# Squares of 32x32 transposed by VectorE for the blocks of w3 and for k and q of pairs 3 to 7

## The chip, the cores and the metric

The kernel runs on one core of a Trainium2 chip. The metric is the device time of one execution in microseconds; the time given is the median of three runs. Beside them one more execution was profiled, and every row below is of that one.

## What is computed

The reference has three parts, one after the other. 

```python
q, k, v: (2, 8, 576, 64) float32; omega: (128, 64)
scale = 1.0 / sqrt(sqrt(64)); q_s, k_s = q * scale, k * scale
phi(x) = exp(x @ omega.T - sum(x*x)/2 - max(...)) / sqrt(128)     # the sum falls out against the max
kv = sum_s phi(k_s)[s, m] * v[s, d];  z = sum_s phi(k_s)[s, m]
attn = (phi(q_s) @ kv) / (phi(q_s) @ z + 1e-6)
x = attn with heads side by side: (1152, 512)
x = ((x @ w1) * (x @ w2)) @ w3 @ w_out             # w1, w2: (512, 1024); w3: (1024, 1024); w_out: (1024, 512); float64
out = sum over 4 experts of p[:, e] * (relu(x @ ew1[e]) @ ew2[e])
```

Since `z` and `kv` divide out the constants, only the product of scale, x and omega enters the exponential. `w3 @ w_out` does not depend on the tokens.

## The kernel before

**Attention.** Batch and head give 16 heads of 576 tokens; two heads are a pair, and eight pairs (0 to 7, class `Pair`) go through the program. A pair's 512 main tokens of k and of q are loaded as a tile of 128 rows by 512 numbers (`kr`, `qr`), transposed, and multiplied with omega (`features`, or `features_halves` from pair 5 on), which VectorE's maximum and ScalarE's exponential turn into `ek` and `eq`. Before, the transposing is done by TensorE: `transposed` (L259) issues four transposes of 128x128 against an identity into a bank, and one copy out of the bank, with the multiplication by the scale, by VectorE for k and by ScalarE for q. The loop over pairs (L514) handles in turn n the features of pair n, the attention of pair n - 1, the transposes of pair n + 1 and the loads of pair n + 2. The tokens over 512 of each head are the tails, loaded and handled apart.

**The fold.** Beside the attention, from the table `BESIDE` (L41), the kernel multiplies w3 by w_out in advance: eight blocks (`fold`, L185), each of two units (`fold_transposed`, L174). A unit is a block of 128 by 512 of w3: loaded as float64 words (`from_f64`, one DMA of 512 KB into a tile with three buffers), made float32 by ScalarE (L93) and VectorE (L94, L95), transposed by TensorE into bank `w`, split into a high part (ScalarE) and a low part (VectorE), and then used as weights of 12 matmuls of 512 columns (L195) into bank `po`. Eight blocks of w_out (`load_wo`) are the right side; they come in the same way and are split by ScalarE and GpSimd.

**After it.** `AFTER` lists the products with w1 and w2 (`gated`, L148; their weights by `load_w12`) and the product with the folded matrix (`expert_input`, L204); then come the experts (L834 and on), which the change leaves alone.

**Order.** The framework's scheduler writes one list of instructions for each engine, by priorities and by its own estimate of times; each engine works through its list in order, so an instruction that waits holds up all that stand behind it on its engine. SP's list holds nearly all the loads. A load by SP takes one of eight completion counters in rotation (DMAHW0 to DMAHW7) and waits until the load that had it before, eight loads back, has landed.

Of the kernel before, what the change touches and what calls it, by code (L numbers as in the profile page):

```python
# [8 lines left out]
F32 = mybir.dt.float32  # L9
BF16 = mybir.dt.bfloat16  # L10
F32R = mybir.dt.float32r
U32 = mybir.dt.uint32
ACTF = mybir.ActivationFunctionType
ALU = mybir.AluOpType
AX = mybir.AxisListType

HI, LO = 0, 1
HS_BUFS = 4
O_BUFS = 6
HALVES = 5  # L20
WARM = 6


# [22 lines left out]
def attention_moe_kernel(ctx: ExitStack, tc: tile.TileContext, q, k, v, omega, mw1, mw2, mw3, mwo, probs, ew1, ew2, out):  # L46
    nc = tc.nc
    B, H, S, D = q.shape
    M = omega.shape[0]
    NT, DM = out.shape  # L50
    DFF = mw1.shape[1]
    NE, _, EFF = ew1.shape
    P = 128
    NPAIR = H // 2
    R = 4
    MAIN = P * R
    TAIL = S - MAIN
    assert B * TAIL == P and B == 2 and H * D == DM and 2 * D == P and M == P
    KD = DM // P
    KF = DFF // P  # L60
    KE = EFF // P
    NTILE = NT // P
    HS = S // 2
    SCALE = float(1.0 / D**0.25)
# [10 lines left out]
    def bank(tag):  # L75
        return ps_p.tile([P, 512], F32, tag=tag, name="ps_" + tag, bufs=BANKS[tag])

    def split(hi, lo, src, eng=None):

        nc.scalar.activation(out=hi, in_=src, func=ACTF.Copy)  # L80
        (eng or nc.vector).tensor_tensor(out=lo, in0=src, in1=hi.bitcast(F32), op=ALU.subtract)  # L81

    def from_f64(src, name):


        r = cv.tile([P, 512, 2], U32, tag="f64", name="f64", bufs=3)
        nc.sync.dma_start(out=r.rearrange("p (k c) w -> p k (c w)", k=src.shape[1]), in_=src.bitcast(U32))
        low, high = r[:, :, 0], r[:, :, 1]
        f = cv.tile([P, 512], F32, tag="f64f", name=name, bufs=2)
        e = cv.tile([P, 512], U32, tag="f64e", name="f64e", bufs=2)  # L90
        fb = f.bitcast(U32)

        nc.scalar.activation(out=f, in_=high.bitcast(F32), func=ACTF.Prelu, scale=2.0**-112, alpha=2.0**32)  # L93
        nc.vector.tensor_scalar(out=e, in0=low, scalar1=29, scalar2=None, op0=ALU.logical_shift_right)  # L94
        nc.vector.scalar_tensor_tensor(out=fb, in0=fb, scalar=3, in1=e, op0=ALU.logical_shift_left, op1=ALU.bitwise_or)  # L95
        return f

    def load_w64(pool, src, name, eng):
        f = from_f64(src, name + "f")
        t = pool.tile([P, 2, 512], F32R, tag=pool.name, name=name)  # L100
        split(t[:, HI], t[:, LO], f, eng=eng)
        return t
# [5 lines left out]
    def transpose(out, in_, rows=slice(0, P)):  # L108
        return nc.tensor.transpose(out, in_, ident[rows, rows])
# [3 lines left out]
    om = const.tile([P, 2, M], F32, name="om")  # L113
# [12 lines left out]

    xt = [[xt_p.tile([P, 2, S], F32R, tag="xt", name=f"xt{i}") for i in range(NPAIR)] for _ in range(B)]


    mctx = ctx.enter_context(ExitStack())  # L130
    w1_p = mctx.enter_context(tc.tile_pool(name="w1", bufs=8, side="right"))
    w3_p = mctx.enter_context(tc.tile_pool(name="w3", bufs=1, side="right"))
    cctx = mctx.enter_context(ExitStack())
    cv = cctx.enter_context(tc.tile_pool(name="cv", bufs=2, side="right"))
    w12, hid, wo, w3o, x2, xf = {}, {}, [], [], {}, {}

    def load_w12(g):

        for w, src in enumerate((mw1, mw2)):
            src = src[:, g * P:(g + 1) * P].rearrange("(k p) c -> p k c", p=P)  # L140
            t = load_w64(w1_p, src, "w12", nc.gpsimd)
            w12[w, g] = t.rearrange("p a (k c) -> p a k c", k=KD)

    def load_wo():
        f = len(wo)
        wo.append(load_w64(w1_p, mwo[f * P:(f + 1) * P].unsqueeze(1), "wo", nc.gpsimd))

    def gated(a_p, bufs, b, g, tags):  # L148

# [23 lines left out]

    def fold_transposed(u):  # L174

        m, hf = divmod(u, KF // 4)
        r = from_f64(mw3[m * P:(m + 1) * P, hf * 512:(hf + 1) * 512].unsqueeze(1), "w3f")
        ps = bank("w")
        for g in range(4):
            transpose(ps[:, g * P:(g + 1) * P], r[:, g * P:(g + 1) * P])  # L180
        wt = cv.tile([P, 2, 512], F32R, tag="w3T", name="w3T", bufs=2)
        split(wt[:, HI], wt[:, LO], ps)
        w3T.append(wt)

    def fold(m):  # L185

        po = bank("po")
        n = 0
        for hf in range(KF // 4):
            u = m * (KF // 4) + hf  # L190
            while len(w3T) < min(u + 2, KF * (KF // 4)):
                fold_transposed(len(w3T))
            for g in range(4):
                for a, c in PASSES:
                    nc.tensor.matmul(  # L195
                        out=po, lhsT=w3T[u][:, a, g * P:(g + 1) * P], rhs=wo[hf * 4 + g][:, c],
                        start=(n == 0), stop=(n == 3 * KF - 1),
                    )
                    n += 1
        t = w3_p.tile([P, 2, 512], F32R, tag="w3o", name="w3o", bufs=KF)  # L200
        split(t[:, HI], t[:, LO], po)
        w3o.append(t)
# [51 lines left out]
    with ExitStack() as actx:  # L254
        at = actx.enter_context(tc.tile_pool(name="at", bufs=2))
# [3 lines left out]
        def transposed(r, name, tag="t"):  # L259

            ps = bank(tag)
            for g in range(4):
                transpose(ps[:, g * P:(g + 1) * P], r[:, 2 * g:2 * g + 2].rearrange("p r d -> p (r d)"))
            t = at.tile([P, 512], F32, tag=name, name=name)
            if name == "kT":
                nc.vector.tensor_scalar(out=t, in0=ps, scalar1=SCALE, scalar2=None, op0=ALU.mult)
            else:
                nc.scalar.activation(out=t, in_=ps, func=ACTF.Copy, scale=SCALE)
            return t

        ended = []
# [51 lines left out]
        def raw_tile(name, bufs=2):  # L323
            return at.tile([P, 2 * R, D], F32, tag=name, name=name, bufs=bufs)
# [5 lines left out]
        ps = bank("po")  # L330
        for n in range(WARM):
            nc.tensor.matmul(out=ps, lhsT=zeros[:, :P], rhs=zeros, start=True, stop=True)
# [4 lines left out]
        ps = bank("x")  # L337
        om_first = transpose(ps[:, :M], om_raw.rearrange("m j d -> m (j d)")).ins
        for j in range(2):
            s = slice(j * D, (j + 1) * D)  # L340
            nc.vector.tensor_copy(out=om[s, j], in_=ps[s, :M])
            nc.gpsimd.tensor_copy(out=omh[s], in_=om[s, j])

        va = [st.tile([P, 2 * R, D1], F32, name=f"va{n}") for n in range(2)]
# [3 lines left out]
        for b in range(B):  # L348
            t = st.tile([P, H, D1], F32, name=f"vt{b}")
# [18 lines left out]
        class Pair:  # L368


            def __init__(self, n):
                self.n, self.b, self.i = n, n // NPAIR, n % NPAIR
                self.ek, self.eq, self.eT = [None] * 2, [None] * 2, [None] * 2

            def load_kq(self, q_eng=nc.sync):
                b, i = self.b, self.i
                self.raw = []
                for name, src, eng in (("kr", k, nc.sync), ("qr", q, q_eng)):
                    r = raw_tile(name)
                    eng.dma_start(  # L380
                        out=r.rearrange("p (h r) d -> p h (r d)", h=2),
                        in_=src[b, 2 * i:2 * i + 2, :MAIN, :].rearrange("h (p r) d -> p h (r d)", r=R),
                    )
                    self.raw.append(r)

            def load_v(self):

# [9 lines left out]
                nc.gpsimd.tensor_copy(out=self.va[:, :, :D], in_=self.vr)  # L397

            def transpose_kq(self):
                self.kT = transposed(self.raw[0], "kT")  # L400
                self.qT = transposed(self.raw[1], "qT", "t" if self.n else "et")

# [8 lines left out]
            def features(self, t, e):  # L411
                if self.n >= HALVES:
                    return features_halves(t, e)
# [4 lines left out]
            def of(self, e, j, r):  # L418

                return e[r % 2][:, 2 * j + r // 2] if self.n >= HALVES else e[j][:, r]  # L420

            def kv_sums(self):

                ps = bank("kv")
                for j in range(2):
                    h = 2 * self.i + j
                    for r in range(R + 1):
                        e, a = (self.of(self.ek, j, r), self.va[:, j * R + r]) if r < R else (ekt[:, h], vt[self.b][:, h])
                        nc.tensor.matmul(out=ps[:, j * D1:(j + 1) * D1], lhsT=e, rhs=a, start=(r == 0), stop=(r == R))
                self.kva = at.tile([P, 2, D1], F32, tag="kva", name="kva", bufs=NPAIR + 1)  # L430
                nc.scalar.activation(out=self.kva, in_=ps[:, :2 * D1].rearrange("p (j d) -> p j d", j=2), func=ACTF.Copy)
# [26 lines left out]
        def attend_tail(b, ps_of):  # L458
# [13 lines left out]
            s = TAIL_COLS  # L472
            for i in range(NPAIR):
                transpose(ps[:, i * P:(i + 1) * P], xs[:, 2 * i:2 * i + 2].rearrange("p j d -> p (j d)"))
            for i in range(NPAIR):
                x, c = xt[b][i], i * P + b * TAIL
                split(x[:, HI, s], x[:, LO, s], ps[:, c:c + TAIL])

        pairs = [Pair(n) for n in range(B * NPAIR)]

# [83 lines left out]
    for s in AFTER.split():  # L564
        if s[0] == "w":
            load_w12(int(s[1]))
        elif s[0] == "c":
            if s == "c0":
                cctx.close()
                xq_p = mctx.enter_context(tc.tile_pool(name="xq", bufs=1, reuse_waits="tile", side="right"))  # L570
            expert_input(int(s[1]))
        else:
            gated(a_p, 6, int(s[1]), int(s[2]), ALL_BANKS[int(s[1])])
# [305 lines left out]
```

## Time and profile before

| | |
|---|---|
| median of three runs | 677.01 us (676.75 to 678.62) |
| the profiled execution | 675.28 us, of which its span is 673.5 us |
| TensorE busy in the span | 98% |
| VectorE, ScalarE, GpSimd busy | 67%, 61%, 18% |

The span runs from the first instruction to the last; the 1.8 us left of the execution lie around it. A share is an average over stages: attention and fold (to about 145 us), the products after them (to about 300 us), and the experts.

### The profile page before, as it was taken

To read this page: it belongs to the slowest core of one execution; us is meant where nothing else is said; L and a number is where in the kernel's file an instruction comes from. 1 tells how busy PE (TensorE), PEld (TensorE's weight loads), DVE (VectorE), ACT (ScalarE), POOL (GpSimd) and SP (SyncE) were. 2 spreads that over 40 slices of the span, in tenths; PEclk is the share of its full clock that TensorE was granted. 3 is DMA by queue.
4 is the path that set the end of the run, shared out by engine and by line. 5 is a ranking of instruction groups with operands and counts; after the bars stand their busy time and mean duration, and the time that the engine had idled before them with its cause. 6 is when DMAs were issued, how large, how long until landed. Compare 5 with 4: busy or idle time off the path is not lost.

```text
span 673.5 us, 12392 instructions
## 1 busy us (share of the span) xinstructions
PE 661.3 (98%) x4895; PEld 634.7 (94%) x4895; DVE 448.9 (67%) x754; ACT 414.1 (61%) x895; POOL 123.9 (18%) x145
## 2 busy tenths in 40 slices
PE   8999999999999999999999999999999999999997
PEld 6788888889999999999899999999999998999996
DVE  3867755657462225257968867968689588687795
ACT  5897465574352224237868778768587677687740
POOL 2321000042140000000022141321331312304300
PEclk9999999999999999999999999999999999999999
DMA  9865333156120002002255385592872765737715
GB/s 230 289 204 173 109 111 95 63 176 200 32 64 1 1 1 64 1 1 64 77 143 142 46 145 108 98 154 48 156 142 32 147 120 83 142 75 105 135 44 172
DMA packets 51178, 70.58 MB, mean 105 GB/s; under 512 B 8048, under 2 KB 34160, under 8 KB 51120
## 3 DMA queue, kind: packets, MB, share of 16 engines
q1 hardware_dynamic: 37792, 49.05, 24.3%
q0 software_dynamic: 12640, 20.19, 20.1%
q8 instruction: 38, 0.62, 0.4%
q10 hardware_dynamic: 688, 0.56, 0.2%
q14 instruction: 20, 0.16, 0.1%
HBM read 47.24 MB, written 22.54 MB: 104 GB/s over the span
## 4 chain that ended last, share of the span: by engine, by line
PE 83%; DMA 5%; DVE 4%; issue 3%; ACT 3%; SPq 1%; POOL 0%; DVEq 0%; ACTq 0%; POOLq 0%
PE ps_po L195 6%; PE ps_f L709 6%; PE ps_f L791 5%; PE ps_x L709 3%; PE ps_w L709 3%; PE ps_et L709 3%; PE ps_po L158 3%; PE ps_f L158 3%; PE ps_kv L709 3%; PE ps_po L709 3%; PE ps_kv L791 3%; PE ps_x L791 3%; PE ps_w L158 3%; PE ps_et L791 3%; PE ps_t L709 2%
## 5 line engine op out<-in xcount | busy, mean ns | idle before, releaser
L743 POOL DMA_DIRECT2D out_dram<-o x98 | 81.9, 912 | 355.2 <-DVE o L768 173.0
L81 DVE TENSOR_TENSOR hs<-hd,hs 128x1024 fp32r<-128x1024 f32 x48 | 58.3, 1218 | 1.5 <-ACT hs L80 1.5
L80 ACT ACTIVATE hs<-hd 128x1024 fp32r<-128x1024 f32 x48 | 50.6, 1056 | 5.7 <-DVE hd L605 4.6
L195 PE MATMUL ps_po<-wo,w3T 128*128 128x512 f32 x192 | 48.3, 400 | 0.0
L709 PE MATMUL ps_f<-x,w1e 128*128 128x288 f32 x288 | 46.2, 294 | 0.0
L693 ACT ACTIVATE hd<-hd 128x288 f32<-128x288 f32 x96 | 40.7, 438 | 9.0 <-DVE hd L691 8.5
L605 DVE TENSOR_TENSOR hd<-hd 128x512 f32<-128x512 f32 x64 | 43.9, 686 | 0.8
L605 DVE TENSOR_TENSOR raw<-raw 128x512 f32<-128x512 f32 x64 | 43.9, 686 | 0.5
L791 PE MATMUL ps_f<-w2e,hs 128*128 128x256 f32 x288 | 43.2, 282 | 0.0
L81 DVE TENSOR_TENSOR w2e<-raw,w2e 128x1024 fp32r<-128x1024 f32 x32 | 38.8, 1218 | 5.4 <-ACT w2e L80 5.3
L195 PEld LDWEIGHTS ps_po<-wo,w3T 128*128 128x128 f32 x192 | 34.8, 188 | 7.0
L709 PEld LDWEIGHTS ps_f<-x,w1e 128*128 128x128 f32 x288 | 40.9, 188 | 0.1
L791 PEld LDWEIGHTS ps_f<-w2e,hs 128*128 128x128 f32 x288 | 38.5, 191 | 0.1
L80 ACT ACTIVATE w2e<-raw 128x1024 fp32r<-128x1024 f32 x32 | 33.1, 1054 | 6.3 <-DVE raw L605 3.2
L81 POOL TENSOR_TENSOR w<-w12f,w 128x512 fp32r<-128x512 f32 x16 | 23.5, 1478 | 68.0 <-ACT w L80 68.0
L81 DVE TENSOR_TENSOR w1e<-raw,w1e 128x1024 fp32r<-128x1024 f32 x24 | 29.3, 1219 | 5.8 <-ACT w1e L80 5.7
L158 PE MATMUL ps_po<-xt,w 128*128 128x288 f32 x144 | 32.5, 296 | 0.4 <-DVE w3o L81 0.4
L158 PE MATMUL ps_w<-xt,w 128*128 128x288 f32 x144 | 32.8, 297 | 0.0
L80 ACT ACTIVATE hid<-a 128x288 fp32r<-128x288 f32 x32 | 12.8, 439 | 28.8 <-DVE a L169 28.8
L80 ACT ACTIVATE w1e<-raw 128x1024 fp32r<-128x1024 f32 x24 | 25.4, 1058 | 6.2 <-issue 2.6
L94 DVE TENSOR_SCALAR f64e<-f 128x512 uint32<-128x512 uint32 x40 | 20.6, 520 | 8.4 <-DMA f<-in_moe_w_dram 5.5
L158 PE MATMUL ps_x<-xt,w 128*128 128x288 f32 x96 | 25.8, 297 | 0.0
(272 smaller groups left out, 1769.2 us busy)
## 6 DMA issues: line engine op xcount, KB each, us to landing
f<-in_moe_w_dram SPq DMA_DIRECT2D x32, 512.0 KB, 3.8
raw<-in_moe_w_dram SPq DMA_DIRECT2D x32, 512.0 KB, 5.2
out_dram<-o POOLq DMA_DIRECT2D x56, 256.0 KB, 5.3
out_dram<-o POOLq DMA_DIRECT2D x42, 128.0 KB, 4.8
f<-in_moe_w_out_dram SPq DMA_DIRECT2D x8, 512.0 KB, 6.2
kr<-in_k_dram SPq DMA_DIRECT2D x8, 256.0 KB, 5.3
vr<-in_v_dram SPq DMA_DIRECT2D x8, 256.0 KB, 4.9
o<-out_dram SPq DMA_DIRECT2D x8, 256.0 KB, 3.8
```

Source lines behind the costliest of these rows:

```text
L80: nc.scalar.activation(out=hi, in_=src, func=ACTF.Copy)
L81: (eng or nc.vector).tensor_tensor(out=lo, in0=src, in1=hi.bitcast(F32), op=ALU.subtract)
L94: nc.vector.tensor_scalar(out=e, in0=low, scalar1=29, scalar2=None, op0=ALU.logical_shift_right)
L158: nc.tensor.matmul(out=bs[c][:, :HS], lhsT=w12[w, g][:, x, kk], rhs=xt[b][kk][:, y, c * HS:(c + 1) * HS], start=(kk == 0 and n == 0), stop ...
L195: nc.tensor.matmul(out=po, lhsT=w3T[u][:, a, g * P:(g + 1) * P], rhs=wo[hf * 4 + g][:, c], start=(n == 0), stop=(n == 3 * KF - 1),)
L605: nc.vector.tensor_tensor(out=o, in0=x, in1=y, op=op)
L693: nc.scalar.activation(out=h, in_=src, func=ACTF.Relu)
L709: nc.tensor.matmul(out=ps, lhsT=w1t[a][:, x, kk, g * P:(g + 1) * P], rhs=x2[b, kk][:, y, s], start=(k in "125" and kk == 0 and n == 0), st ...
L743: dma = nc.gpsimd.dma_start(out=out[toks, d], in_=src[rows], **({} if fresh else dict(accum_op=ALU.add))).ins
L791: nc.tensor.matmul(out=ps, lhsT=t[a][:, x, g, j * P:(j + 1) * P], rhs=w2t[b][:, y, g], start=(k in "15" and g == 0 and n == 0), stop=(k in ...
```

## The change

1. Each block of w3 is loaded by four DMAs, one for each group of 32 partitions, each of which takes 32 rows of four column pieces. VectorE's 32x32 transpose of the tile (one instruction for 128x512, within partition groups) then gives the block transposed, and the split reads and writes it with reordered columns. Four TensorE transposes for each unit and their use of bank `w` go. The rows of w3 in a group of weights are others than before, so w_out's blocks are loaded with matching rows, also in four DMAs.
2. k and q of pairs 3 to 7 are loaded by eight DMAs for a tile of 256 KB, in runs of 32 numbers (128 bytes), and transposed by one VectorE instruction from SBUF to SBUF. Pairs 0 to 2 and the tails stay with TensorE.
3. The scale is multiplied into omega once, so the copies out of the banks no longer multiply.
4. Folded blocks alternate between banks `po` and `w`.

```diff
+SQUARES = 3
...
-    def from_f64(src, name):
+    def from_f64(srcs, name):
         r = cv.tile([P, 512, 2], U32, tag="f64", name="f64", bufs=3)
-        nc.sync.dma_start(out=r.rearrange("p (k c) w -> p k (c w)", k=src.shape[1]), in_=src.bitcast(U32))
+        rows = P // len(srcs)
+        for i, src in enumerate(srcs):
+            o = r[i * rows:(i + 1) * rows].rearrange("p (k c) w -> p k (c w)", k=src.shape[1])
+            nc.sync.dma_start(out=o, in_=src.bitcast(U32))
...
     def load_wo():
-        f = len(wo)
-        wo.append(load_w64(w1_p, mwo[f * P:(f + 1) * P].unsqueeze(1), "wo", nc.gpsimd))
+        hf, g = divmod(len(wo), 4)
+        first = [hf * 512 + i * P + g * SQ for i in range(4)]
+        wo.append(load_w64(w1_p, [mwo[f:f + SQ].unsqueeze(1) for f in first], "wo", nc.gpsimd))
...
     def fold_transposed(u):
         m, hf = divmod(u, KF // 4)
-        r = from_f64(mw3[m * P:(m + 1) * P, hf * 512:(hf + 1) * 512].unsqueeze(1), "w3f")
-        ps = bank("w")
-        for g in range(4):
-            transpose(ps[:, g * P:(g + 1) * P], r[:, g * P:(g + 1) * P])
+        rows = mw3[m * P:(m + 1) * P].rearrange("(j r) f -> r j f", r=SQ)
+        first = [hf * 512 + i * P for i in range(4)]
+        r = from_f64([rows[:, :, f:f + P] for f in first], "w3f")
+        t = cv.tile([P, 512], U32, tag="f64e", name="w3t", bufs=2).bitcast(F32)
+        nc.vector.transpose(t, r)
+        t = t.rearrange("p (j g r) -> p g j r", j=4, g=4)
         wt = cv.tile([P, 2, 512], F32R, tag="w3T", name="w3T", bufs=2)
-        split(wt[:, HI], wt[:, LO], ps)
+        hi, lo = (wt[:, x].rearrange("p (g j r) -> p g j r", j=4, g=4) for x in (HI, LO))
+        split(hi, lo, t)
         w3T.append(wt)
 
     def fold(m):
-        po = bank("po")
+        po = bank(("po", "w")[m % 2])
...
             if name == "kT":
-                nc.vector.tensor_scalar(out=t, in0=ps, scalar1=SCALE, scalar2=None, op0=ALU.mult)
+                nc.vector.tensor_copy(out=t, in_=ps)
             else:
-                nc.scalar.activation(out=t, in_=ps, func=ACTF.Copy, scale=SCALE)
+                nc.scalar.activation(out=t, in_=ps, func=ACTF.Copy)
+            return t
+
+        def load_squares(t, src, eng):
+            t = t.rearrange("p n d -> p (n d)").rearrange("p (h g q c) -> p h g q c", h=2, g=2, c=SQ)
+            src = src.rearrange("h (q p g j) (i c) -> h j i p g q c", q=4, g=2, j=2, c=SQ)
+            for n in range(4):
+                for h in range(2):
+                    eng.dma_start(out=t[n * SQ:(n + 1) * SQ, h], in_=src[h, n // 2, n % 2])
+
+        def squares(r, name):
+            t = at.tile([P, 512], F32, tag=name, name=name)
+            nc.vector.transpose(t, r.rearrange("p n d -> p (n d)"))
             return t
...
-            nc.vector.tensor_copy(out=om[s, j], in_=ps[s, :M])
+            nc.vector.tensor_scalar(out=om[s, j], in0=ps[s, :M], scalar1=SCALE, scalar2=None, op0=ALU.mult)
...
+                self.squares = n >= SQUARES
...
+                    if self.squares:
+                        load_squares(r, src[b, 2 * i:2 * i + 2, :MAIN], eng)
+                        continue
...
             def transpose_kq(self):
+                if self.squares:
+                    self.kT, self.qT = (squares(r, name) for r, name in zip(self.raw, ("kT", "qT")))
+                    return
```

**SP's list, from the first w_out block to the loads of pair 3.** In rows of SP's list, `f_...` is the tile of float64 words, and the brackets name what the row waits for. Before, from the load of v of pair 2 on:

```order
L391 DMA vr<-in_v_dram 128x2x256 [waits DMAHW7_49,Pool_49]
L87 DMA f_247<-in_moe_w_out_dram 128x1024 [waits DMAHW0_49]
L87 DMA f_257<-in_moe_w_out_dram 128x1024 [waits DMAHW1_49]
L87 DMA f_267<-in_moe_w_out_dram 128x1024 [waits DMAHW2_49]
L391 DMA vr<-in_v_dram 128x2x256 [waits DMAHW3_49,Pool_49]
L380 DMA kr<-in_k_dram 128x2x256 [waits DMAHW4_49,PE_49]
L380 DMA qr<-in_q_dram 128x2x256 [waits DMAHW5_49,PE_49]
```

Now the same place, where the pattern of four rows for a w_out block goes on for two more blocks:

```order
L421 DMA vr<-in_v_dram 128x2x256 [waits DMAHW7_49,Pool_49]
L92 DMA f_247<-in_moe_w_out_dram 32x1024 [waits DMAHW0_49]
L92 DMA f_247<-in_moe_w_out_dram 32x1024 [waits DMAHW1_49]
L92 DMA f_247<-in_moe_w_out_dram 32x1024 [waits DMAHW2_49]
L92 DMA f_247<-in_moe_w_out_dram 32x1024 [waits DMAHW3_49]
...
L290 DMA kr<-in_k_dram 32x8x32 [waits DMAHW4_49,PE_49]
L290 DMA kr<-in_k_dram 32x8x32 [waits DMAHW5_49]
```

Between the load of v of pair 2 and the end of the loads of q of pair 3 stood 6 loads and now stand 28; up to the second block of w3 it is 74, and over the stage w_out, w3, k and q take 176 loads in place of 34.

**VectorE's list at the attention of pair 1.** `xs` is the attention's output of a pair, `d` its divisor, `wof` a block of w_out. Before:

```order
L364 TENSOR_TENSOR xs<-ps_w,d 128x4x64
L362 TENSOR_SCALAR d<-ps_po 128x4
L363 RECIPROCAL d<-d 128x4
L364 TENSOR_TENSOR xs<-ps_po,d 128x4x64
L95 SCALAR_TENSOR_TENSOR wof<-wof,f64e 128x512
```

Now:

```order
L390 TENSOR_TENSOR xs<-ps_w,d 128x4x64
L294 STREAM_TRANSPOSE kT<-kr 128x512
L388 TENSOR_SCALAR d<-ps_po 128x4
L389 RECIPROCAL d<-d 128x4
L390 TENSOR_TENSOR xs<-ps_po,d 128x4x64
L100 SCALAR_TENSOR_TENSOR wof<-wof,f64e 128x512
```

The transpose of k of pair 3 has come to stand among the rows of pair 1; it waits for a DMA, where the copy that it replaces stood nine rows further down and waited for TensorE.

**TensorE's list at the second block of the fold.** `w3T` is a split unit. Before:

```order
L109 MATMUL ps_w<-ident,w3f 128x128 x4
L303 MATMUL ps_f<-omh,kT 128x128 x5
L109 MATMUL ps_t<-ident,qr 128x128 x2
L195 MATMUL ps_po<-wo,w3T 128x512 x12
L109 MATMUL ps_x<-ident,xs 128x128 x4
```

Now:

```order
L208 MATMUL ps_po<-wo,w3T 128x512 x24
L114 MATMUL ps_x<-ident,xs 128x128 x4
L499 MATMUL ps_kv<-kva,eTt 128x65 x4
L329 MATMUL ps_f<-omh,kT 128x128 x5
L208 MATMUL ps_w<-wo,w3T 128x512 x12
```

The transposes of w3 and of q are gone, the two units of a block stand closer together, and the second block goes to bank `w`.

## Rows read from the trace of the kernel before

**Rows 1.** Page, busy time in us, share of the span, instructions.

```profile
PE 661.3 (98%) x4895; PEld 634.7 (94%) x4895; DVE 448.9 (67%) x754; ACT 414.1 (61%) x895; POOL 123.9 (18%) x145
```

**Rows 2.** Stretches of the span: busy us by engine, clock, DMA share, GB/s.

```profile
12.00:28.00 16.00, 15.16 (x105) 13.35 (x104) 11.88 (x22) 13.80 (x41) 4.52 (x5) 1.00 1.04 342
28.00:52.00 24.00, 21.80 (x139) 18.04 (x138) 16.91 (x34) 22.71 (x65) 6.28 (x6) 1.00 0.64 200
60.00:142.00 82.00, 82.00 (x566) 71.55 (x565) 50.09 (x110) 45.47 (x117) 2.71 (x4) 1.00 0.33 97
142.00:165.00 23.00, 22.63 (x168) 21.87 (x168) 17.17 (x41) 13.98 (x29) 10.12 (x7) 1.00 0.75 240
165.00:300.00 135.00, 135.00 (x1018) 135.00 (x1017) 52.88 (x109) 46.27 (x106) 11.90 (x8) 1.00 0.07 21
300.00:673.00 373.00, 366.54 (x2806) 359.93 (x2804) 288.59 (x418) 261.02 (x511) 81.88 (x98) 1.00 0.54 107
```

**Rows 3.** Chain that ended last, 56 to 165 us: start, us, what.

```profile
80.37 0.44 PE ps_w L109 x4
80.81 2.77 PE ps_po L195 x12
```

**Rows 4.** The same chain, 0 to 56 us.

```profile
12.69 7.29 DMA f<-in_moe_w_out_dram
...
44.88 5.91 DMA f<-in_moe_w_dram
```

**Rows 5.** Groups by form, TensorE, whole span: busy us, mean ns.

```profile
L109 PE MATMUL ps_w<-ident,w3f 128*128 128x128 f32 x64 | 10.2, 276 | 0.0
```

**Rows 6.** Groups by form, TensorE, 52 to 143 us.

```profile
L109 PE MATMUL ps_t<-ident,qr 128*128 128x128 f32 x8 | 1.4, 281 | 0.0
L109 PE MATMUL ps_t<-ident,kr 128*128 128x128 f32 x8 | 1.2, 272 | 0.0
```

**Rows 7.** Groups by form, VectorE and ScalarE, whole span.

```profile
L81 DVE TENSOR_TENSOR w1e<-raw,w1e 128x1024 fp32r<-128x1024 f32 x24 | 29.3, 1219 | 5.8 <-ACT w1e L80 5.7
L94 DVE TENSOR_SCALAR f64e<-f 128x512 uint32<-128x512 uint32 x40 | 20.6, 520 | 8.4 <-DMA f<-in_moe_w_dram 5.5 <-DMA f<-in_moe_w_out_dram 2.2
L95 DVE SCALAR_TENSOR_TENSOR w3f<-w3f,f64e 128x512 uint32<-128x512 uint32 x16 | 10.9, 682 | 0.0
L268 ACT ACTIVATE qT<-ps_t 128x512 f32<-128x512 f32 x8 | 5.0, 629 | 0.5 <-PE ps_f L279 0.3 <-PE ps_t L109 0.2
```

**Rows 8.** VectorE in order of time: start, us, instruction.

```profile
24.02 0.15 DVE L362 TENSOR_SCALAR d<-ps_po 128x4 f32<-128x4 f32 x1
...
48.55 0.68 DVE L285 TENSOR_REDUCE mx<-ps_f 128x4 f32<-128x512 f32 x1
49.15 0.68 DVE L95 SCALAR_TENSOR_TENSOR wof<-wof,f64e 128x512 uint32<-128x512 uint32 x1
```

**Rows 9.** SP in order of time.

```profile
4.41 3.58 SPq L321 DMA_DIRECT2D vt<-in_v_dram  x2
...
11.71 1.41 SPq L87 DMA_DIRECT2D f<-in_moe_w_out_dram  x3
...
60.88 5.38 SPq L580 DMA_DIRECT2D pr<-in_moe_domain_probs_dram  x10
```

**Rows 10.** DMA issues: KB each, median us from issue to landing.

```profile
f<-in_moe_w_dram SPq DMA_DIRECT2D x32, 512.0 KB, 3.8
...
kr<-in_k_dram SPq DMA_DIRECT2D x8, 256.0 KB, 5.3
...
tail<-in_k_dram SPq DMA_DIRECT2D x2, 128.0 KB, 6.0
...
om_raw<-in_omega_dram ACTq DMA_DIRECT2D x1, 32.0 KB, 2.0
```

**Rows 11.** Three short stretches, columns as in Rows 2.

```profile
9.00:10.00 1.00, 0.56 (x5) 0.56 (x6) 0.77 (x2) 1.00 (x5) 0.39 (x1) 1.00 1.28 145
16.00:18.00 2.00, 2.00 (x20) 2.00 (x19) 0.59 (x2) 1.57 (x6) 0.00 (x0) 1.00 1.03 410
65.00:67.00 2.00, 2.00 (x10) 1.67 (x9) 0.52 (x1) 2.00 (x6) 0.00 (x0) 1.00 0.14 4
```

More of the change, by code (lines that the diff above doesn't have):

```diff
@@ L53, in attention_moe_kernel @@
     P = 128
+    SQ = 32
     NPAIR = H // 2
@@ L96, in from_f64, with load_w64 @@
         return f
-    def load_w64(pool, src, name, eng):
-        f = from_f64(src, name + "f")
+    def load_w64(pool, srcs, name, eng):
+        f = from_f64(srcs, name + "f")
         t = pool.tile([P, 2, 512], F32R, tag=pool.name, name=name)
@@ L140, in load_w12 @@
             src = src[:, g * P:(g + 1) * P].rearrange("(k p) c -> p k c", p=P)
-            t = load_w64(w1_p, src, "w12", nc.gpsimd)
+            t = load_w64(w1_p, [src], "w12", nc.gpsimd)
             w12[w, g] = t.rearrange("p a (k c) -> p a k c", k=KD)
     def load_wo():
-        f = len(wo)
-        wo.append(load_w64(w1_p, mwo[f * P:(f + 1) * P].unsqueeze(1), "wo", nc.gpsimd))
+        hf, g = divmod(len(wo), 4)
+        first = [hf * 512 + i * P + g * SQ for i in range(4)]
+        wo.append(load_w64(w1_p, [mwo[f:f + SQ].unsqueeze(1) for f in first], "wo", nc.gpsimd))
     def gated(a_p, bufs, b, g, tags):
@@ L379, in load_kq @@
                     r = raw_tile(name)
+                    self.raw.append(r)
+                    if self.squares:
+                        load_squares(r, src[b, 2 * i:2 * i + 2, :MAIN], eng)
+                        continue
                     eng.dma_start(
@@ L383, in load_kq @@
                     )
-                    self.raw.append(r)
             def load_v(self):
```

## Prediction

> **What bounds the kernel now.** I read the shares first: TensorE is busy 98% of the span [rows 1]. That is an average, so I cut the span into stages [rows 2]. From 60 to 142 us TensorE is busy 82.00 of 82.00 us while VectorE has 50.09 and ScalarE 45.47; from 165 to 300 us it has no idle time either. Between 12 and 52 us this is otherwise: ScalarE is busy 22.71 of 24 us from 28 to 52, the DMA engines are full (share 1.04) from 12 to 28, and the chain that ended last runs through two DMA waits of 7.29 and 5.91 us [rows 4]. After 56 us the chain is TensorE's own work in sequence, a group of four transposes (0.44 us) and then a unit of the fold (2.77 us) [rows 3]. So the kernel has a start of some 52 us that loads and ScalarE set, and from there TensorE sets the time. TensorE's work taken away behind 52 us is gained in full as long as its inputs keep up; work taken away ahead of it is gained only through ScalarE or the loads.
>
> **TensorE's work removed.** The 64 transposes of w3 [rows 5] all lie behind 52 us, and of those of k and q 16 do [rows 6]. A busy time of 276 ns overlaps with its neighbours; what one costs in a full engine is its part of the chain, 0.44 / 4 = 0.11 us [rows 3]. 80 x 0.11 = 8.8 us, term A = -8.8. The other 24 transposes (2.6 us, pairs 3 to 5) lie in the start, where TensorE is not the limit: between 0 and 2.6, I take 0. The alternating banks free nothing that shows: TensorE has no idle time between units. The multiplication moved into omega changes no copy's duration that I can see.
>
> **ScalarE's work removed.** Five copies of q of 629 ns go [rows 7]. Two, of pairs 3 and 4, lie between 28 and 52 us, where ScalarE is the fullest engine: term B = -1.2, between 0 (if the loads set the pace there) and -1.2.
>
> **The loads.** SP issues three loads in 1.41 us, 0.47 us apart; ten in 5.38 us, 0.54 apart [rows 9]. The list of SP now holds 74 loads from the first block of w_out to the second of w3: 74 x 0.47 = 34.8 us, from 11.7 to 46.5 us, and with 3.8 us to land [rows 10] that block is there at 50.3. Before, the wait for it ended at 44.88 + 5.91 = 50.8 [rows 4]. So the flood just fits. At 0.54 it ends at 51.7 + 3.8 = 55.5 us, nearly 5 us late. One place is tighter. k of pair 3 comes after 20 loads, 11.7 + 9.4 = 21.1, and lands 2.0 us (32 KB alone) to 5.3 us (256 KB in the crowd) later [rows 10], at 23.1 to 26.4. Its transpose stands in VectorE's list ahead of the row that began at 24.02 [rows 8]; late, it holds the rest of pair 1's attention, the blocks of w_out and all maxima behind it. q of pair 3, the next w_out blocks and pair 4 follow at the same spacing, so the delays do not add up but shift together. Term C = +2.5, from the two ends 0 and 6, a little below the middle since the start also has slack that absorbs part. Behind 52 us the last w3 loads are issued by about 97 to 110 us, ahead of their use.
>
> Do 128-byte runs fill the DMA engines? No row has one. A tiny packet (16 bytes, the only traffic then) bounds it from below: 0.14 x 16 engines x 2 us = 4.5 us for about 3.7 loads of 128 packets [rows 9, 11], 9.5 ns each. The stretch with 256-byte packets bounds it from above: 145 GB/s over 16 engines at share 1.28 is 7.1 GB/s, 36 ns a packet [rows 11]. A tile of k has 2048 packets, 128 for each engine: 1.2 to 4.6 us, against 256 KB at 410 GB/s = 0.64 us [rows 11]. Ten tiles add 6 to 40 us of engine time over some 80 us that had a share of 0.64 and less [rows 2]. Covered, except near the upper end in the start, which C's upper end holds.
>
> The Trainium skill speaks against such loads: its page "DMA: Bandwidth & Descriptors", section "Rules for kernel authors", calls a plain DMA with a rearranged access pattern 19 times slower than the hardware transpose. Taken at its word, a tile would take 19 x 0.64 = 12 us by that rule, ten 122 us, and the time would come near 740 us; no row here shows it, and its sister passage in "VectorE: DVE Perf Modes", section "The three transpose paths", ties it to a large innermost step, where here 32 numbers lie together.
>
> **VectorE's work added.** It gets 16 transposes of w3 and, in place of copies, those of k and q (for q five more). The trace has no such instruction. The nearest row is one of the same size from SBUF to SBUF, 682 ns; the ends are 520 ns (single input) and 1219 ns (twice the elements, as though each passed twice) [rows 7]. I take 682, a spacing of 0.60 us when back to back [rows 8]. In the stretch 60 to 142 us VectorE then has 50.1 + 18 x 0.60 = 61 us in 73: 83% in place of 61%. It is not the limit, but its list is fixed and each unit now passes VectorE four times (two conversions, transpose, low part) instead of three, so a unit that comes late holds features and divisors behind it. Term D = +1.5, between 0 and 7 (the latter at 1219 ns: 50.1 + 18 x 1.2 = 72 us in 73).
>
> The skill's page "VectorE: DVE Perf Modes", section "The three transpose paths", gives 311 ns for a 128x128 bf16 transpose. Four of these would be 1.24 us, an estimate from that page with nothing of it fixed; D would be 7 by it, and the sum near no change.
>
> **Sum.** -8.8 - 1.2 + 2.5 + 1.5 = -6.0 us, from the profiled execution's 675.3 to 669.3. The median of the runs stood 1.7 us above that execution, so I predict 671.0 us, 0.9% faster. About 0.3% (2 us) is what a measurement of this kernel can tell from no change.
>
> **Rivals.** *Nothing is late.* C and D are 0 and part of the start's transposes counts: 675.3 - 8.8 - 1.2 - 1 = 664.3, plus 1.7 = 666. For it: SP's flood fits at 0.47, and VectorE keeps 17% free. Against: the places above with no slack. *VectorE becomes the limit.* If the transpose takes the 1.2 us of its upper end, D is 7: 675.3 - 10 + 2.5 + 7 = 674.8, median 676.5, no change. It decides from about 1.1 us for one. Against it: the instruction reads one tensor and writes one, like those of 520 to 682 ns. *SP's counters pace the loads: slower.* A load waits until the one eight places back has landed. In the old list this shows where two loads took 3.58 us to issue [rows 9]. From a landing time of 8 x 0.47 = 3.8 us on, SP's spacing is landing / 8. The loads of the tails, 256-byte runs in a full queue, took 6.0 us [rows 10]; at that, 0.75 us x 74 = 55.5 us, the second w3 block is there at 11.7 + 55.5 + 6.0 = 73 us, 22 us late. The fold cannot start, and the time is 675.3 - 10 + 22 + 1.5 + 1.7 = 690. It loses more than 10 us, and turns the sign, from a landing time of about 4.8 us. For it: landings of 5.3 us for k now. Against it: the loads are 32 and 128 KB, not 256 and 512, spread out in time, and 32 KB alone landed in 2.0 us.
>
> **Chances.** Forecast (668 to 675) 0.52; nothing late (below 668) 0.18; VectorE the limit (675 to 679) 0.13; counters pace the loads (above 679) 0.17. So faster by over 0.3% (below 675) 0.70, within 0.3% 0.13, slower 0.17. The range 665.5 to 679 leaves about 0.03 below and 0.17 above; the forecast's own is 668 to 675.
>
> **What would show it.** No idle time of TensorE between the fold's first unit and its last, and that stretch 8 to 10 us shorter, shows A; idle time there that ends on VectorE's low part of `w3T` shows D, on a DMA of w3 the counters. VectorE waiting for a DMA of `kr` near 24 us shows C, and SP's rows show its spacing: about 0.47 us is my case, 0.6 or more the slow rival. The transpose's mean near 0.68 us is the row taken. From 165 us on every stage should last as before. Most likely to make it wrong are the landing time of the small loads and the transpose's duration, neither of which has a row.

## The result: slower, 681.35 us against 675.55

In 19 runs each, the changed kernel took 681.35 us in the median (677.79 to 687.15), the kernel before 675.55 (673.09 to 678.62). The ratio is 1.0093, 95% interval 1.0076 to 1.0109: 5.8 us slower. I had forecast 671.0 us, 6.0 below a median of 677.01 from three runs; over 19 runs the kernel before stands 1.5 us lower than that, so the forecast misses by 11.8 us and not by 10.3.

The profile of the kernel after is of its fastest run, 677.79 us with a span of 676.0 (before 675.3 and 673.5), so the two traces account for 2.5 of the 5.8 us. First its page, which answers [rows 1]: busy time, and the share of each engine in the chain that ended last; the third line is the same chain in the kernel before.

```profile
PE 654.3 (97%) x4791; PEld 625.0 (92%) x4791; DVE 462.5 (68%) x775; ACT 412.5 (61%) x890; POOL 122.8 (18%) x145
...
PE 72%; DVE 7%; DMA 6%; SPq 6%; ACT 5%; issue 3%; POOL 0%; DVEq 0%; ACTq 0%
...
PE 83%; DMA 5%; DVE 4%; issue 3%; ACT 3%; SPq 1%; POOL 0%; DVEq 0%; ACTq 0%; POOLq 0%
```

TensorE lost work as meant: 661.3 - 654.3 = 7.0 us less. But its idle time rose from 673.5 - 661.3 = 12.2 us to 676.0 - 654.3 = 21.7 us, 9.5 more. SP's queue, 1% of the chain before, is 6% now. The stretches, which answer [rows 2], say where (busy us of TensorE, weight load, VectorE, ScalarE, GpSimd; granted clock; DMA share; GB/s):

```profile
12.00:28.00 16.00, 14.54 (x99) 12.61 (x98) 8.89 (x19) 11.71 (x34) 3.29 (x3) 1.00 0.70 164
28.00:52.00 24.00, 19.94 (x116) 16.67 (x116) 14.99 (x29) 18.77 (x57) 5.00 (x5) 0.93 0.61 133
60.00:142.00 82.00, 77.15 (x494) 64.75 (x493) 62.55 (x136) 47.68 (x124) 3.13 (x4) 0.98 0.68 142
142.00:165.00 23.00, 22.00 (x155) 20.69 (x154) 19.23 (x33) 13.01 (x24) 10.74 (x8) 1.00 0.72 213
165.00:300.00 135.00, 135.00 (x1020) 135.00 (x1019) 53.77 (x114) 46.86 (x109) 11.89 (x8) 1.00 0.09 29
```

From 165 to 300 us nothing changed. From 12 to 52 all engines do less than before, ScalarE 18.77 us in place of 22.71, and the DMA engines are no fuller: everybody waits. From 60 to 142 TensorE has 4.85 us of idle time where it had none.

SP in order of time answers [rows 9]:

```profile
11.59 8.01 SPq L92 DMA_DIRECT2D f<-in_moe_w_out_dram  x12
19.70 5.26 SPq L290 DMA_DIRECT2D kr<-in_k_dram  x8
25.06 5.17 SPq L290 DMA_DIRECT2D qr<-in_q_dram  x8
...
52.65 6.50 SPq L92 DMA_DIRECT2D f<-in_moe_w_dram  x12
59.24 5.19 SPq L290 DMA_DIRECT2D kr<-in_k_dram  x8
64.48 5.70 SPq L290 DMA_DIRECT2D qr<-in_q_dram  x8
70.27 0.55 SPq L421 DMA_DIRECT2D vr<-in_v_dram  x1
70.93 7.77 SPq L92 DMA_DIRECT2D f<-in_moe_w_dram  x16
```

Rows follow one another almost without a gap: SP has a load to issue all the time. A load of k or q in squares takes 5.26 / 8 = 0.66 us of it, one of w3 7.77 / 16 = 0.49. What SP itself waited for from 9 to 60 us comes to some 5 us; the four largest (us in total, times, longest):

```profile
SPq L92 <- DMA qr<-in_q_dram: 1.2, 1, 1.2
SPq L92 <- DVE f64e L99: 1.1, 2, 0.8
SPq L92 <- DMA vr<-in_v_dram: 0.7, 1, 0.7
SPq L421 <- POOL va L427: 0.5, 1, 0.5
```

In the kernel before the same view has 15.4 us of waits for TensorE's transposes of k and q alone, and 36 us on engines in all: SP had time to spare there, and now has next to none.

```profile
SPq L380 <- PE ps_t L109: 15.4, 7, 5.1
```

The loads of k and q land quickly, those of w3 and w_out later (KB each, median us to landing; answers [rows 10]):

```profile
f<-in_moe_w_dram SPq DMA_DIRECT2D x64, 128.0 KB, 4.4
f<-in_moe_w_out_dram SPq DMA_DIRECT2D x32, 128.0 KB, 3.8
kr<-in_k_dram SPq DMA_DIRECT2D x40, 32.0 KB, 2.8
qr<-in_q_dram SPq DMA_DIRECT2D x40, 32.0 KB, 2.4
```

How a late load becomes idle time of TensorE is seen twice. VectorE in order of time (answers [rows 8]; in brackets its idle time and what ended it):

```profile
26.95 0.71 DVE L294 STREAM_TRANSPOSE kT<-kr 128x512 f32<-128x512 f32 x1 [1.13 <-DMA qr<-in_q_dram]
...
35.10 0.69 DVE L311 TENSOR_REDUCE mx<-ps_f 128x4 f32<-128x512 f32 x1 [1.88 <-PE ps_f L305]
35.71 0.70 DVE L294 STREAM_TRANSPOSE qT<-qr 128x512 f32<-128x512 f32 x1
```

k of pair 3 is transposed only at 26.95 us, behind a wait for a DMA (the profile names q's; k's own last load was issued at about 24.3 and lands some 2.8 us later). It stands ahead of the row that had begun at 24.02 [rows 8], which now begins at 27.58. In the fold, the chain that ended last runs through the 16 loads of k and q as SP issues them one by one, then the w3 load that stands behind them, its conversion and transpose, to TensorE (start, us, what):

```profile
59.89 0.61 SPq L290
...
69.56 0.61 SPq L290
...
72.32 3.78 DMA f<-in_moe_w_dram
...
76.26 0.69 ACT w3f L98
76.98 0.70 DVE w3f L100
77.70 0.14 DVE w3t L191
...
80.06 0.61 DVE w3T L83
80.71 3.35 PE ps_w L208 x7
```

And behind these two idle stretches TensorE ran at its lower clock level (columns as in the stretches above):

```profile
28.00:32.00 4.00, 1.98 (x9) 1.10 (x8) 2.24 (x5) 2.99 (x10) 1.26 (x1) 1.00 0.42 60
32.00:36.00 4.00, 3.01 (x9) 2.46 (x10) 2.12 (x4) 2.17 (x9) 0.61 (x1) 0.59 1.01 263
...
76.00:80.00 4.00, 1.91 (x16) 1.49 (x14) 3.42 (x9) 2.22 (x5) 0.00 (x0) 1.00 1.08 226
80.00:84.00 4.00, 3.29 (x8) 2.61 (x9) 4.00 (x11) 2.67 (x6) 0.00 (x0) 0.57 0.89 154
```

After 4 us in which it was busy 1.98 and 1.91 us, the granted clock is 0.59 and 0.57, near the 1.2 GHz level, for most of the next 4. What was executed there would have taken some 3.01 x 0.41 + 3.29 x 0.43 = 2.6 us less at the full clock, an estimate from these rows. Of TensorE's 654.3 us, 654.3 - 2.6 = 651.7 are then work at the full clock, 9.6 less than before. So the two spans differ by -9.6 (work) + 9.5 (idle time) + 2.6 (clock) = 2.5 us.

The new transposes themselves, as groups by form (answers [rows 7]):

```profile
L191 DVE STREAM_TRANSPOSE w3t<-w3f 128x512 f32<-128x512 f32 x16 | 11.2, 699 | 0.1
L294 DVE STREAM_TRANSPOSE qT<-qr 128x512 f32<-128x512 f32 x5 | 3.5, 708 | 1.4 <-DMA vr<-in_v_dram 1.4
L294 DVE STREAM_TRANSPOSE kT<-kr 128x512 f32<-128x512 f32 x5 | 3.5, 699 | 1.1 <-DMA qr<-in_q_dram 1.1
```

### The profile page after: what moved, and what is told of

Same layout as the page of the kernel before. It is cut to its first block, busy times and chain, and to the rows that moved or that the text cites. A ratio compares the mean times of both kernels' runs of the same rounds, so it can differ in the third digit from the quotient of the medians.

```text
span 676.0 us, 12441 instructions
## 1 busy us (share of the span) xinstructions
PE 654.3 (97%) x4791; PEld 625.0 (92%) x4791; DVE 462.5 (68%) x775; ACT 412.5 (61%) x890; POOL 122.8 (18%) x145
## 4 chain that ended last, share of the span: by engine, by line
PE 72%; DVE 7%; DMA 6%; SPq 6%; ACT 5%; issue 3%; POOL 0%; DVEq 0%; ACTq 0%
PE ps_f L742 6%; PE ps_f L824 6%; SPq L290 4%; PE ps_x L742 3%; PE ps_w L742 3%; PE ps_et L742 3%; PE ps_kv L742 3%; PE ps_t L742 3%; PE ps_po L742 3%; PE ps_x L824 3%; PE ps_et L824 3%; PE ps_t L824 3%; PE ps_kv L824 3%; DMA f<-in_moe_w_dram 3%; PE ps_w L824 2%
## 5 line engine op out<-in xcount | busy, mean ns | idle before, releaser
L166 PE MATMUL ps_w<-xt,w 128*128 128x288 f32 x144 | 34.2, 298 | 0.6 <-DVE a L177 0.6
L208 PE MATMUL ps_w<-wo,w3T 128*128 128x512 f32 x96 | 26.4, 421 | 2.8 <-DVE w3T L83 2.8
L166 PEld LDWEIGHTS ps_w<-xt,w 128*128 128x128 f32 x144 | 24.9, 188 | 0.8 <-DVE a L177 0.8
L166 PEld LDWEIGHTS ps_po<-xt,w 128*128 128x128 f32 x144 | 25.2, 189 | 0.1
```

What stands on the lines that cost most here:

```text
L166: nc.tensor.matmul(out=bs[c][:, :HS], lhsT=w12[w, g][:, x, kk], rhs=xt[b][kk][:, y, c * HS:(c + 1) * HS], start=(kk == 0 and n == 0), stop ...
L208: nc.tensor.matmul(out=po, lhsT=w3T[u][:, a, g * P:(g + 1) * P], rhs=wo[hf * 4 + g][:, c], start=(n == 0), stop=(n == 3 * KF - 1),)
```

## The experiments

The theory: SP's list has become the pacer; 70 more loads for k and q and 72 for w_out and w3 make each load late, and TensorE's idle time and low clock eat what the transposes give. Rivals: VectorE's added work; the 128-byte packets on the DMA engines. "In squares" means loaded in pieces and transposed by VectorE in squares of 32x32. Each time stands beside that of the kernel before, measured along with it.

**Only w3 in squares.** `SQUARES = 8` in place of 3.

> Squares for w3 alone: k and q of all pairs come as they did before and are transposed by TensorE, so 80 loads of 128-byte runs (0.655 us of SP each in the kernel after, 52 us in all) become 20 loads; TensorE takes back 16 transposes. If SP's list paces the kernel after (the theory), the first fold matmul is back near 59 us and the time is 667 to 670 us, some 6 to 8 us below before. If VectorE's added work is the cause (16 of its 26 added transposes stay), most of the loss stays: 675 us or more. If 128-byte packets load the DMA engines, the same 667 to 670 us, and the third kernel tells these two apart.

673.04 us against 674.65, ratio 0.9982 (0.9963 to 1.0). The loss is gone, so it came with k and q; VectorE's 16 transposes of w3 don't make it. But the gain was 1.6 us, hardly clear of none, and not 6 to 8, and the first fold matmul came at 64.5 us, not 59. Its stretches from 28 to 52 and from 60 to 142 us, and the first and last start of the fold's matmuls (ns least, median, most; us):

```profile
28.00:52.00 24.00, 23.35 (x135) 19.81 (x134) 14.71 (x30) 20.20 (x58) 6.01 (x7) 0.87 0.73 191
60.00:142.00 82.00, 81.75 (x530) 70.56 (x529) 62.14 (x127) 48.23 (x121) 4.78 (x5) 0.99 0.45 117
...
L208 PE MATMUL ps_po<-wo,w3T x96: 387/393/501, 64.5 to 127.8; 128*128 128x512 f32 x96
```

The fold starts almost as late as in the kernel after (65.4 us), and yet TensorE is idle for 0.25 us from 60 to 142, and not for 4.85: the fold's start does not tell the two kernels apart, the idle time behind it does. From 28 to 52 us the clock is low here too, 0.87, in a profiled run of 676.49 us.

**Only k and q in squares.** w_out, w3 and the fold's bank as before.

> Squares for k and q of pairs 3 to 7 alone; w3 and w_out load as before and w3 is transposed by TensorE. If SP's list paces it (the theory), the 80 loads delay the start by several us, and the time is 678 to 684 us, slower than before. If VectorE's added work is the cause, it has only 10 of the 26 transposes more, and the time is within 2 us of before (674 to 678 us).

683.32 us, ratio 1.0122 (1.0101 to 1.0144), 8.7 us slower: as the theory has it, and against VectorE as the cause. The two parts, -1.6 and +8.7, add up to +7.1; together they gave +5.8.

**q's squares from GpSimd's queue.**

```
load_squares(r, src[...], nc.gpsimd if name == "qr" else eng)
```

> The kernel after, with q's 40 square loads issued from GpSimd's queue in place of SP's: the same packets on the DMA engines, the same work of VectorE, SP relieved of some 25 us of issues. If SP's list paces the kernel after (the theory), the time falls to 668 to 675 us. If the cause is VectorE's work or the 128-byte packets, it stays at 680 to 682 us.

683.48 us, ratio 1.0124 (1.0104 to 1.0144): no relief. The expectation failed. That need not speak for the rivals: GpSimd makes the low parts of w_out, and these now stand in its list among the loads. The group of `wo` on GpSimd in this kernel (ns least, median, most; first and last start, us):

```profile
L83 POOL TENSOR_TENSOR wo<-wof,wo x8: 1267/1289/1346, 35.0 to 76.3; 128x512 fp32r<-128x512 f32 x8
```

In the kernel after the last of them began at 60.1 us; here at 76.3, and the fold's first block, which needs all eight blocks of w_out in turn, began at 83.1 us. That fits a wait moved to another list. But TensorE's clock from 60 to 100 us was lower as well (0.79, in the kernel after 0.96), and this run doesn't separate the two.

**Loads cut, nothing else.** First those of k and q of pairs 3 to 7 in the kernel before, in eight; then those of w_out and w3, in four:

```
 for x in range(8):
     rows = slice(x * 16, (x + 1) * 16)
     eng.dma_start(out=r.rearrange(...)[rows], in_=src[...].rearrange(...)[rows])
...
+rows = P if src.shape[1] > 1 else 32
+for i in range(0, P, rows):
+    nc.sync.dma_start(out=o[i:i + rows], in_=src[i:i + rows].bitcast(U32))
```

> The kernel before, with each of the ten loads of k and q of pairs 3 to 7 cut into eight loads of 1 KB runs; TensorE transposes all, VectorE has nothing more. If SP's list paces the kernel after (the theory), this alone slows the kernel before: 70 loads more at some 0.42 us each are 29 us of SP, and the time is 677 to 683 us. If the number of loads costs nothing, it is that of before within 0.3%.

> The kernel before, with the loads of w_out and w3 cut into four by partitions (rows of 4 KB stay whole); TensorE transposes all, VectorE has nothing more. If the number of loads on SP's list costs by itself (the theory), the start of the fold is 3 to 6 us late, and the time is 677 to 681 us. If not, it is that of before within 0.3%.

686.0 us against 674.65, ratio 1.0165 (1.0145 to 1.0186), and 679.43 us against 674.63, ratio 1.0065 (1.0048 to 1.0082): 11.4 and 4.8 us slower, the first beyond its expected 683, with TensorE's transposes, no 128-byte run and nothing new on VectorE. This is the core of the answer: the number of loads costs by itself, and neither rival is needed for it. One thing goes with the number: the scheduler orders the lists anew for each kernel, so this price holds that of the new order too. By difference these two also price the transposes, as an estimate: squares of w3 against as many loads without them, 673.04 - 679.43 = -6.4 us, 0.10 us for each of 64; for k and q 683.32 - 686.0 = -2.7 us, though the loads there are slower ones. In the second kernel the first fold matmul is at 64.0 us:

```profile
L198 PE MATMUL ps_po<-wo,w3T x192: 387/393/497, 64.0 to 150.2; 128*128 128x512 f32 x192
```

**Loads that carry nothing.** The kernel before, each load in one piece, and beside each of them as many loads of 4 bytes on SP as the cut had added.

```
+def extra(n):
+    for _ in range(n):
+        i = len(spared)
+        spared.append(i)
+        nc.sync.dma_start(out=spare[:, i:i + 1], in_=omega[:1, i % 64:i % 64 + 1])
```

> The kernel before, with every load of w_out and w3 in one piece as it was, and three loads of 4 bytes into an unused column issued on SP beside each: the number of issues of the run with the loads cut in four, next to no bytes and no packets, and no piece that anything waits for. If SP's issue time is the cost (the theory), this is as slow as that run, 677 to 681 us. If what costs is that a tile is there only when its fourth piece has landed, or the transfers of the pieces, it is that of before, 673 to 676 us.

> The kernel before, with every load of k and q of pairs 3 to 7 in one piece as it was, and seven loads of 4 bytes into an unused column issued on SP beside each: the number of issues of the run in which these loads were cut into eight. If SP's issue time is the cost (the theory), 681 to 687 us, as in that run. If the pieces themselves cost, 673 to 677 us.

678.83 us against 675.06, ratio 1.0052 (1.0032 to 1.0071), and 683.01 us, ratio 1.0126 (1.01 to 1.0152): 3.8 and 8.0 us slower, 79% and 70% of what the cut loads cost. So most of it needs no bytes, no packets and no tile that is whole only with its last piece. Not all of it is issue time, though. SP from 9 to 60 us in the second kernel, in order of time, and what it waited for:

```profile
12.94 5.46 SPq L89 DMA_DIRECT2D spare<-in_omega_dram  x7
...
42.93 2.17 SPq L89 DMA_DIRECT2D spare<-in_omega_dram  x7
```

```profile
SPq L89 <- DMA f<-in_moe_w_out_dram: 9.3, 6, 3.3
SPq L89 <- DMA f<-in_moe_w_dram: 3.5, 3, 1.8
```

Seven such loads take 2.17 us when SP waits for nothing, 0.31 each, and 5.46 us where they wait for older loads of w_out to land. These waits on transfers come to 17 us there (10 us in the kernel with k and q cut) and to 2.5 us in the kernel after. A further load thus has two prices on SP, its issue and the wait for an older one; in the kernel after it is nearly all issue. The order moved here too: the load of v of pair 3, ahead of k's and q's in the kernel before (13.42 us), now stands behind them (24.32 us). No run here separates the two.

**Where the pieces stand.** Three tries to save the w3 part, all with k and q loaded as before: the first four units of w3 in one load and by TensorE; w_out's blocks 1, 3, 4 beside pairs 0, 1, 2 in place of 3, 2, 3; half of w_out's pieces from GpSimd's queue. A control has the second shift in the kernel before.

> The kernel with squares for w3 alone, whose first four units of w3 are loaded in one piece each and transposed by TensorE as before (their columns put into the order of the new w_out rows while they are made to f32); the other twelve units by VectorE. SP has 12 loads fewer before the fold starts, but w_out still comes in 32 pieces. If SP's list up to the fold's start is what counts (the theory), the first fold matmul comes before 64.5 us, nearer to 59, and the time is 668 to 672 us, though 16 of the 64 transposes of w3 are back on TensorE (1.8 us). If VectorE's or the DMA engines' added work in the fold is what eats the gain, it stays at 672 to 675 us.

> Squares for w3 alone, with the eight blocks of w_out loaded 1, 3 and 4 beside the attention of pairs 0, 1 and 2, in place of 3, 2 and 3: the four-piece loads leave SP's list ahead of k of pair 3, where the split alone was seen to delay it. If the place of the pieces in SP's list costs (the theory), the idle of TensorE at 24 to 28 us and the low clock after it go, and the time is 667 to 671 us. If the pieces cost wherever they stand (DMA engines, later blocks late instead), it stays at 672 to 676 us.

> Squares for w3 alone, with two of the four pieces of each w_out block issued from GpSimd's queue: the same pieces at the same points of the program, 16 fewer on SP's list. If SP's issues are what costs (the theory), 668 to 672 us. If the pieces cost as such, on the DMA engines, 672 to 676 us; if GpSimd's own list is held up by waits for a free buffer, more than that.

> Control: the kernel before with only the same shift of w_out's loads (1, 3, 4 in place of 3, 2, 3 blocks), each in one piece. If the shift is worth something by itself the time falls by the same amount as in the first kernel of this call; the theory says it is worth little here, since one-piece loads take SP 1.4 us for three blocks: that of before within 2 us.

676.09 us against 674.63 (ratio 1.0018, 1.0001 to 1.0034); 677.15 against 674.99 (1.0034, 1.0011 to 1.0057); 673.66 (0.9977, 0.9951 to 1.0002); the control 673.4 (0.9982, 0.9969 to 0.9995). The first two came out above all that was expected of them, the third where the pieces cost as such. The theory in this narrow form, that one place in SP's list costs, fell: the first fold matmul stayed at 64.6 and 64.5 us in the first two, and no version beat the simplest one, squares of w3 alone, clear of noise. The idle at 24 to 28 us did go in the second, and came back at 50 to 54. The control says one thing more. Its fold began later than that of the kernel before, and it was 1.6 us faster: the fold's start alone is no measure of the time.

```profile
L195 PE MATMUL ps_po<-wo,w3T x192: 387/393/500, 59.0 to 145.1; 128*128 128x512 f32 x192
...
L195 PE MATMUL ps_po<-wo,w3T x192: 387/393/501, 61.2 to 145.6; 128*128 128x512 f32 x192
```

**Squares of k and q late only.** The first of these kernels with pairs 6 and 7 in squares.

> The same, and k and q of pairs 6 and 7 in squares (32 loads of 128-byte runs in place of 4, SP 0.655 us each: 18 us more of SP, late in the attention). If a load costs time only where SP's list is what the next stage waits for (the theory), this loses 2 to 5 us against the kernel of the run before it (670 to 676 us); if VectorE's transposes cost, four of them take 2.8 us of VectorE and lose at most 1 us; if neither, it gains 0.9 us, eight transposes on TensorE.

681.39 us, ratio 1.0096 (1.0074 to 1.0117): 5.3 us more than without, just above the 2 to 5 us of the theory, for 28 loads more and four transposes of VectorE. The range given, 670 to 676, was missed, since the kernel that it was counted from had come out at 676.09.

**Filling TensorE's gaps.** Thirty matmuls of zeros that nothing reads, in the kernel with w3 alone, in the kernel after, and in the one with half of w_out's pieces on GpSimd.

```
+def fill(ps, n):
+    for _ in range(n):
+        nc.tensor.matmul(out=ps, lhsT=zeros[:, :P], rhs=zeros, start=True, stop=True)
```

> Squares for w3 alone, with zero matmuls on TensorE that nothing reads (128x512 bf16, one ahead of each of the first 20 feature halves, two ahead of the k sums of the first five pairs, each into the bank that the next matmul overwrites): 30 matmuls, some 6.5 us of TensorE at the full clock, part of it in its idle gaps. If the low clock after TensorE's idle is part of the loss (the theory: the runs of this kernel without them had a mean clock of 0.994, 0.6% of 674 us or 4 us), the clock rises to 0.998 or more and the time falls to 668 to 672 us, less what the matmuls add where TensorE was not idle. If the clock has another cause, it stays at 0.994 and the time rises by 1 to 5 us, to 674 to 678 us.

> The same zero matmuls in the kernel after, whose runs had a mean clock of 0.991 (0.9% of 674 us, 6 us). If idle brings the low clock (the theory), the clock rises to 0.996 or more and the time falls by 2 to 5 us, to 676 to 679 us, still not below before, since the late loads stay. If not, the time rises to 682 to 686 us.

> The same zero matmuls in the kernel with squares for w3 alone and half of w_out's pieces on GpSimd's queue, whose twelve runs went from 670.1 us at a mean clock of 0.999 to 679.7 us at 0.987. If idle brings the low clock, the spread closes towards its low end, 670 to 673 us. If not, 675 to 679 us.

676.17 us against 674.24 (ratio 1.0019, 0.9992 to 1.0046), 687.52 (1.018, 1.0132 to 1.0229) and 677.23 (1.0032, 1.0009 to 1.0055). They failed: the mean clock rose a little in the first, from 0.994 to 0.996, and fell in the second, from 0.991 to 0.988, and all three are slower than without, by 3.1, 6.2 and 3.6 us. In the third the spread did close, but at its upper end (675.63 to 678.9). The matmuls cost more than they gave back. What the low clock costs by itself stays open. That it matters is only seen side by side: the 19 runs of the kernel after had mean clocks of 0.985 to 0.995, those of the kernel before, where they are recorded, 0.999 in the mean, and the run at 0.985 that took 687.15 us is 9.4 us longer than the one of 677.79 at 0.994.

## Why the prediction was wrong

The terms for what might come late, C and D, were forecast at 4.0 us together; TensorE's idle time grew by 9.5, and a lower clock, which no term held, took 2.6 more.

**TensorE's work removed (A, -8.8): right.** By the profile TensorE does 9.6 us less at the full clock, and against the cut loads alone the w3 part is worth 6.4 us, where 64 x 0.11 is 7.0. The condition that I set, "as long as its inputs keep up", is what failed.

**VectorE (D, +1.5): right in the instruction's time.** The transposes took 699 to 708 ns, where I took 682; VectorE was busy 62.55 us from 60 to 142, where I had 61 in a stretch of 73. What D itself cost was not measured alone; for w3 the difference above leaves 7.0 - 6.4 = 0.6 us, less than the noise of the two runs. The estimate from the Trainium skill, page "VectorE: DVE Perf Modes", section "The three transpose paths", was 1.24 us; the trace does not agree. The 2.8 us that TensorE waited for `w3T` in the fold would be VectorE's by the mark that the prediction set; the chain above leads back from there to a w3 load and SP's issues, so the mark was too coarse.

**The loads (C, +2.5, at most 6): the step that failed.** It said "So the flood just fits", from 74 loads at 0.47 us, and the second w3 block there at 50.3 us. The spacing 0.47 came from loads of another shape. Those of k and q in 128-byte runs took 0.66, and w_out's first twelve pieces 8.01 / 12 = 0.67, their waits included; the second w3 block was issued at about 52.65 + 8 x 0.54 = 57.0 and landed some 4.4 us later, at 61 us. The list was mis-sized, then, by 11 us at this point. The tighter place, k of pair 3, which I had at 23.1 to 26.4 us, came at 26.95. The fold started 6.4 us late (65.4 us against 59.0), but that is not yet the loss: with w3 alone it started at 64.5, without a loss. About half of the new idle time, 4.85 us, lies from 60 to 142 us, and there the step failed as well: I wrote that behind 52 us the w3 loads come ahead of their use, and the 16 loads at 59.24 to 70.2 us made one late that TensorE needed at 78. Even the bound from 0.54 would have put the block at 55.5 us and C near 5; the row was there, and I took the more favourable one.

**A term was missing**: the lower clock behind idle stretches, 2.6 us in the profiled run, whose mean clock was 0.994 (before 0.999). Over the 19 runs it was 0.991, which by the same measure is some 4 us, an estimate.

**ScalarE (B, -1.2): nothing came of it**, since the start was no longer ScalarE's: it had 5 us of idle time between 28 and 52.

**The rivals.** The slower one, SP's counters, had the right place (SP's list) and a mechanism that here cost little: its condition was a landing of 3.8 us or more for these loads. The pieces of w_out and w3 met it with 3.8 and 4.4 us, those of k and q, in 2.8 and 2.4 us, did not, and SP's waits for landings came to 2.5 us from 9 to 60. SP was held by the issues themselves. The mark that I gave it, a spacing of "0.6 or more", was met by the loads of k and q, without that mechanism. Its price was too high: the fold started 6.4 us late, not 22, and its stretch was still 3.1 us shorter (the prediction's mark for A was 8 to 10). First and last start of its matmuls:

```profile
L208 PE MATMUL ps_po<-wo,w3T x96: 387/389/499, 65.4 to 137.6; 128*128 128x512 f32 x96
...
L208 PE MATMUL ps_w<-wo,w3T x96: 387/395/795, 73.2 to 148.4; 128*128 128x512 f32 x96
```

Before, they started from 59.0 to 145.1 us. The DMA engines' own time for 128-byte runs was covered in the start, as said: their share from 28 to 52 us was 0.61, before 0.64. From 60 to 142 it doubled, 0.68 against 0.33, and was 1.08 where TensorE waited (76 to 80 us); the w3 load of the chain still landed in 3.78 us. By the estimate from the Trainium skill, page "DMA: Bandwidth & Descriptors", section "Rules for kernel authors", a tile would have taken 12 us; here one took 5.26 us to issue and 2.8 to land, 8.1 in all, and what cost was the issuing, of which that sentence doesn't speak.

## What to carry to other kernels

Before a transpose is moved into the loads, count the loads on the queue that issues them, and price each by a row of the same shape; where there is none, take the slow end, and ask what the queue has to spare (here 36 us of waits on engines before, 3 us after). An issuing queue that is never idle is a bound like an engine, though no busy share names it: it shows as rows without gaps and as consumers that wait for different loads in turn. Cutting a change into its loads alone, with the old computation, told cause from bystander, and two runs with loads that carry nothing told number from bytes.

## What was not expected of the hardware

The time that SP takes for one load depends on its shape: 0.66 us for 32 KB in 128-byte runs, 0.49 for a w3 piece of 1 KB runs, 0.31 for 4 bytes when nothing is waited for. A load of 4 bytes can hold SP for several us: those above waited up to 3.3 us for older loads of w_out to land. In the kernel after, TensorE's granted clock fell to 0.59 and 0.57 behind two stretches in which it had been busy 1.98 and 1.91 of 4 us, and added matmuls that nothing reads did not raise that kernel's mean clock (0.988, without them 0.991).
